# Shared k/q buffer, two accumulators, one PSUM tile for den and num, and a split first wave in a fused attention and gated FFN kernel

## Chip, cores and metric

One core of one Trainium2 chip. The metric is device time in microseconds (us), the median over several executions. All kernels here were checked against the reference and were correct.

## The reference, cut to what matters

Polynomial sketch attention over 4 batches of 4 heads and 1088 rows, followed by a gated FFN on all 4352 tokens:

```python
def phi(x):                      # r = 8, so 64 features
    a = np.einsum('rd,bhsd->bhsr', S1, x)
    b = np.einsum('rd,bhsd->bhsr', S2, x)
    return np.einsum('bhsi,bhsj->bhsij', a, b).reshape(*x.shape[:-1], r * r)
q_p, k_p = phi(q), phi(k)
kv  = np.einsum('bhsf,bhsd->bhfd', k_p, v)
z   = np.sum(k_p, axis=2)
num = np.einsum('bhsf,bhfd->bhsd', q_p, kv)
den = np.einsum('bhsf,bhf->bhs', q_p, z)[..., None] + 1e-06
x   = num / den                  # then (B,H,S,D) -> (B*S, 128)
gate = 1.0 / (1.0 + np.exp(-(x @ w_gate)))          # d_ff = 1536
out  = (gate * (x @ w_val)) @ w_out
```

## The kernel before

TensorE does FFN *waves* (gate and value product of one block of 128 FFN columns, for 512 tokens) and *output matmuls*, and the attention of the next batch is slipped in between them with `slot(group, waves)`. den and num stand in tiles of two different PSUM pools:

```python
    def den(b, n):
        dps = ps1.tile([P, 512], F32, tag="one", name="dps")
        for h in range(H):
            nc.tensor.matmul(out=dps[32 * h : 32 * h + 32, :w], ...)
        def invert():
            nc.vector.transpose(out=dT[:, :tn]..., in_=dps[:, :w])
            ...                                    # rc, reciprocal, rb
        return invert

    def num(b, n):
        nps = ps2.tile([P, 2, 512], F32, tag="two", name="nps")
        ...                                        # 4 heads x 2 halves of matmuls
        def divide():                              # xT <- nps * rb
            ...
        return divide
```

Names in the profile lines: kT and qT are k and q transposed; kps and cqps are the matmuls that sketch k and q; qp and bq are the two factors of the features of q, written to DRAM (dq) and read back repeated, and their product goes into qp. kvz, ndps, zb and nd lead to kv and z. dT is den transposed, rc its reciprocal, rb the reciprocal spread out, and xT the quotient that the FFN reads. sg is the sigmoid, g the gated product, moeout the output accumulator.

The order on the queues for a batch, and the narrowing of weights to float32 (`w_sb`), of which the last step needs a square from ScalarE and a sum from GpSimd:

```python
    def num0_den1(b):
        divide = num(b, 0)
        invert = den(b, 1)
        divide()
        invert()
    ...                                            # for batches 1 to 3
        qmult(b, 0)                                # qp <- qp * bq (bq: repeated operand)
        slot(lambda: ndt(b), wn)
        qmult(b, 1)
        slot(lambda: den(b, 0)(), wn)
        slot(lambda: num0_den1(b), wn + 1)
        slot(lambda: num(b, 1)(), 3)

        # in narrow():
        nc.scalar.activation(out=cap.bitcast(F32), in_=cap.bitcast(F32), func=ACTF.Square)
        nc.gpsimd.tensor_tensor(out=head, in0=head, in1=tail, op=ALU.add)
        yield
        nc.vector.scalar_tensor_tensor(
            out=out, in0=cap.bitcast(F32), scalar=1.265625 * 2.0**-30, in1=head.bitcast(F32), ...)
```

Of the kernel before, what the change touches and what calls it, by code (L numbers as in the profile page):

```python
# [9 lines left out]
I32 = mybir.dt.int32  # L10
# [10 lines left out]
def kernel(  # L21
# [42 lines left out]
    ps1 = ctx.enter_context(tc.tile_pool(name="ps1", bufs=1, space=bass.MemoryType.PSUM))  # L64
# [18 lines left out]
    def narrow(out, bits, eng):  # L83




        n, m = out.shape[1:]
        lo, hi = bits[:, :, :, 0].bitcast(U32), bits[:, :, :, 1]

        def tmp(dt, tag, bufs):
            return sbN.tile([P, 3, P], dt, tag=tag, name=tag, bufs=bufs)[:, :n, :m]



        cap, tail = tmp(I32, "cap", 5), tmp(I32, "tail", 4)
        eng.tensor_scalar(  # L97
            out=cap.bitcast(F32), in0=hi.bitcast(F32), scalar1=122880.0, scalar2=-122880.0,
            op0=ALU.min, op1=ALU.max,
        )  # L100
        nc.scalar.activation(out=tail, in_=lo, func=ACTF.Copy, scale=2.0**-29)  # L101
        yield

        head = tmp(I32, "head", 3)
        nc.vector.tensor_scalar(  # L105
            out=head, in0=cap, scalar1=3, scalar2=0x3FFFFFF8,
            op0=ALU.logical_shift_left, op1=ALU.bitwise_and,
        )
        nc.vector.scalar_tensor_tensor(  # L109
            out=head, in0=cap, scalar=-0x40000000, in1=head, op0=ALU.bitwise_and, op1=ALU.bitwise_or  # L110
        )
        yield
        nc.scalar.activation(out=cap.bitcast(F32), in_=cap.bitcast(F32), func=ACTF.Square)  # L113
        nc.gpsimd.tensor_tensor(out=head, in0=head, in1=tail, op=ALU.add)  # L114
        yield

        nc.vector.scalar_tensor_tensor(  # L117
            out=out, in0=cap.bitcast(F32), scalar=1.265625 * 2.0**-30, in1=head.bitcast(F32),
            op0=ALU.is_ge, op1=MUL,
        )  # L120
        yield
# [39 lines left out]
    def narrow_w(j, step):  # L161
        if not 0 <= j < NJ:
            return
        n, jj = divmod(j, 2)
        if wide:
            if step == 0:
                narrowing[j] = narrow(w_sb[:, :, j, :], w_in[n][:, :, jj], nc.gpsimd)
            next(narrowing[j])


    def load_rows(src, b, tag, parts=((0, T, nc.sync),), t=None):
        if t is None:
            t = ld.tile([P, T, D], F32, tag=tag, name=tag)
# [9 lines left out]
        return t  # L183
# [16 lines left out]
    k_t[0] = load_rows(k, 0, "k", ((0, KBASE[2] + 1, nc.scalar), (KBASE[2] + 1, T, nc.sync)))  # L200
    q_t[0] = load_rows(q, 0, "q", ((0, T0, nc.sync),))
    v_t[0] = load_v(0)
    load_w(0)
    load_rows(q, 0, "q", ((T0, T, nc.sync),), q_t[0])
    for n in range(1, 4):
        load_w(n)

    def load_kq(b):
        if b < B:
            k_t[b] = load_rows(k, b, "k")  # L210
            q_t[b] = load_rows(q, b, "q")

    k_t[1] = load_rows(k, 1, "k")
    for n in range(4, NJ // 2):
        load_w(n)
    v_t[1] = load_v(1)
    q_t[1] = load_rows(q, 1, "q")
# [32 lines left out]
    def w2(ci, j0, jn, g):  # L250
        t0, tw = tok_chk[ci]
        if j0 == 0:
            moe["acc"] = pso.tile([P, TCH], F32, tag="moeout", name="moeout")
# [33 lines left out]
    def w1():  # L287
# [6 lines left out]
        for which in range(2):  # L294
            for jj in range(jn):
                nc.tensor.matmul(  # L296
                    out=wv[:, which, jj * tw : (jj + 1) * tw],
                    lhsT=w_sb[:, which, j0 + jj, :],
                    rhs=xT[:, t0 : t0 + tw],
                    start=True,  # L300
                    stop=True,
                )
        sg = sbG.tile([P, TCH], F32, tag="sg", name="sg", bufs=3)
        nc.scalar.activation(out=sg, in_=wv[:, 0], func=ACTF.Sigmoid)  # L304
        if ci == 0:
            narrow_w(j0 + 4, 0)
            if j0 == 0:
                narrow_w(1, 3)
            narrow_w(j0 + 2, 1)
            narrow_w(j0 + 2, 2)  # L310
            if j0 > 0:
                narrow_w(j0 + 1, 3)
# [18 lines left out]
    def slot(group, waves):  # L331
# [4 lines left out]
        for _ in range(waves):  # L336
# [7 lines left out]
            lag = 3 if last or todo and todo[0][1] == 0 and todo[0][0] > 0 else 2  # L344
            while len(todo) >= lag:
                w2(*todo.pop(0))
                lag = 3 if last else 2
# [115 lines left out]
    def qcomp(b, ns, pool):  # L463
# [23 lines left out]
        BQ[b] = sbA.tile([P, H * TP * 32], F32, tag="bq", name="bq", bufs=1)  # L487
# [44 lines left out]
    def kv(b, j_list, zsum=None):  # L532

        if b not in KVZ:
            KVZ[b] = ps1.tile([P, 512], F32, tag="one", name="kvz")
        kvz = KVZ[b]
        for j in j_list:
            kr = 64 if j == 0 else P
            for which in range(2 if zsum is None else 1):
                for h in range(H):  # L540
                    nc.tensor.matmul(  # L541
                        out=kvz[32 * h : 32 * h + 32, F * which : F * which + F],
                        lhsT=v_t[b][:kr, h, j, :] if which == 0 else ones[:kr, :],
                        rhs=KP[b][:kr, h // 2, j, h % 2, :],
                        start=(j == 1 and which == 0),
                        stop=(j == 0),
                        skip_group_check=True,
                    )
        if 0 not in j_list:
            return  # L550
        if zsum is not None:
            for h in range(H):
                nc.tensor.matmul(
                    out=kvz[32 * h : 32 * h + 32, F : 2 * F],
                    lhsT=ones,
                    rhs=zsum[:, h, :],
                    start=False,
                    stop=True,
                    skip_group_check=True,
                )  # L560

        KVD[b] = sbA.tile([P, 2, 2, F], F32, tag="kvd", name="kvd")
        k0 = kvz[:, : 2 * F]
# [25 lines left out]
    def ndt(b, pool=(ps1, "one")):  # L589
        ndps = pool[0].tile([P, 2, 256], F32, tag=pool[1], name="ndps")  # L590
# [16 lines left out]
    def den(b, n):  # L607
        t0, tn = q_chk[n]
        w = 32 * tn
        dps = ps1.tile([P, 512], F32, tag="one", name="dps")  # L610
        for h in range(H):
            nc.tensor.matmul(  # L612
                out=dps[32 * h : 32 * h + 32, :w],
                lhsT=zb[b % 2][:, h, :],
                rhs=half(QP[b], n)[:, 2 * (h % 2) + h // 2, :],
                start=True,
                stop=True,
            )

        def invert():  # L620

            dT = sbA.tile([P, 9, 32], F32, tag="dT", name="dT")
            nc.vector.transpose(out=dT[:, :tn].rearrange("p t c -> p (t c)"), in_=dps[:, :w])  # L623
            rc = sbA.tile([P, 9, 2], F32, tag="rc", name="rc")
            nc.vector.tensor_scalar_add(rc[:, :tn], dT[:, :tn, :2], 1e-6)
            nc.vector.reciprocal(out=rc[:, :tn], in_=rc[:, :tn])

            rb = sbA.tile([P, 9, 2, 32], F32, tag="rb", name="rb")
            r0 = rc[:, :tn]
            nc.vector.transpose(  # L630
                out=rb[:, :tn].rearrange("p t c s -> p (t c s)"),
                in_=bass.AP(
                    tensor=r0.tensor, offset=r0.offset, ap=[list(r0.ap[0]), [1, 2 * tn], [0, 32]]
                ),
            )
            RB[b, n] = rb

        return invert

    def num(b, n):  # L640
        t0, tn = q_chk[n]
        w = 32 * tn
        nps = ps2.tile([P, 2, 512], F32, tag="two", name="nps")
        for h in range(H):
            for c in range(2):
                rows = slice(64 * c, 64 * c + 64)
                nc.tensor.matmul(  # L647
                    out=nps[32 * h : 32 * h + 32, c, :w],
# [6 lines left out]
        def divide():  # L655
            o = b * S + 64 * t0
            nc.vector.tensor_tensor(  # L657
                out=xT[:, o : o + 2 * w].rearrange("p (t c s) -> p c t s", c=2, s=32),
                in0=nps[:, :, :w].rearrange("p c (t s) -> p c t s", s=32),
                in1=RB[b, n][:, :tn].rearrange("p t c s -> p c t s"),  # L660
                op=MUL,
            )
            moe["ready"] = o + 2 * w
# [40 lines left out]
    for j0, j1 in ((0, 5), (5, NJK)):  # L704
        for pi in range(2):
            outer(0, pi, j0, j1)
        if j0 == 0:
            kv(0, [1, 2, 3, 4])
    narrow_w(0, 0)
    kv(0, [5, 6, 7, 8, 0])  # L710
    narrow_w(1, 0)
    mult00()
    narrow_w(0, 1)
    mult10()
    narrow_w(0, 2)
    ndt(0, (pso, "moeout"))
    warm(256)
    narrow_w(0, 3)
    invert = den(0, 0)
    divide = num(0, 0)  # L720
    warm(512)
    narrow_w(2, 0)
    narrow_w(3, 0)
    invert()
    divide()
    narrow_w(1, 1)
    narrow_w(1, 2)
    turn_q(0, 1)
# [10 lines left out]
    def num0_den1(b):  # L739
        divide = num(b, 0)  # L740
        invert = den(b, 1)
        divide()
        invert()

    def q01():
        spread(0, (1,), qcomp(0, (1,), (ps2, "two")), nc.scalar, True)

    slot(q01, 6)
    qmult(0, 1)
    slot(None, 2)  # L750
    slot(lambda: den(0, 1)(), 1)
    slot(lambda: num(0, 1)(), 1)
    for b in range(1, B):
# [7 lines left out]
        load_kq(b + 1)  # L761
# [6 lines left out]
        slot(lambda: kv(b, [1, 2, 3, 4, 5, 6, 7, 8, 0], ZS[b]), wn)  # L768
# [5 lines left out]
        slot(lambda: den(b, 0)(), wn)  # L774
        slot(lambda: num0_den1(b), wn + 1)
        slot(lambda: num(b, 1)(), 3)
# [31 lines left out]
```

## Time and profile before

| | before |
|---|---|
| time, median of 3 (range); a fourth execution came with the result | 315.51 us (314.66 to 316.38) |
| span of the profiled execution | 313.1 us, granted clock 0.999 |
| TensorE busy | 300.3 us (96%) |
| first wave starts | 18.05 us |
| two gaps before an output matmul, both for g | 1.33 us at 40.92, 1.13 us at 81.41 |

TensorE is the bound, so what counts is where it waits. From its timeline alone: a wave takes 1.715 us when nothing holds it, an output step of two matmuls 0.8575 us, and there are 102 of each, 262.4 us in all.

### The profile page before, as it was taken

How to read it: one execution, taken by the hardware profiler on the slowest of the kernel's cores; microseconds unless marked ns; L12 is line 12 of the kernel's file. 1: busy time of each engine (PE TensorE's matmuls, PEld its weight loads, DVE VectorE, ACT ScalarE, POOL GpSimd, SP SyncE). 2: the span in 40 equal slices, each digit the busy share in tenths (PEclk: the TensorE clock that was granted, in tenths of full speed). 3: DMA queues.
4: the chain of work that ended last, by engine and by line, in shares of the span. 5: the costliest groups of instructions: out<-in, count | busy, mean ns of one | idle time of the engine just before them, and what ended most of it. 6: DMA issues, size and time to landing. Idle time of an engine off the chain costs nothing.

```text
span 313.1 us, 3666 instructions
## 1 busy us (share of the span) xinstructions
PE 300.3 (96%) x1394; PEld 135.5 (43%) x1394; DVE 155.0 (49%) x259; ACT 80.9 (26%) x149; POOL 21.2 (7%) x34
## 2 busy tenths in 40 slices
PE   7889989999799999999999999999999999999994
PEld 2423423453244444543443444433444444444683
DVE  4888798843827444465246451653332223222331
ACT  2445532321122122212222222312122222222220
POOL 1256621000000000000000000000000000000000
PEclk9999999999999999999999999999999999999999
DMA  7996302596204393220003750110002000200011
GB/s 180 345 380 200 118 1 75 149 158 128 66 0 108 101 171 119 60 51 1 2 0 55 173 116 13 16 20 0 0 0 34 0 2 2 32 0 0 8 28 17
DMA packets 28656, 22.91 MB, mean 73 GB/s; under 512 B 19808, under 2 KB 23776, under 8 KB 28640
## 3 DMA queue, kind: packets, MB, share of 16 engines
q1 hardware_dynamic: 27712, 22.14, 28.3%
q10 hardware_dynamic: 928, 0.54, 0.7%
q8 instruction: 11, 0.18, 0.2%
q14 instruction: 5, 0.04, 0.0%
HBM read 19.46 MB, written 3.21 MB: 72 GB/s over the span
## 4 chain that ended last, share of the span: by engine, by line
PE 77%; DMA 11%; DVE 5%; SPq 4%; issue 1%; POOL 1%; ACT 1%; DVEq 0%; POOLq 0%; ACTq 0%
PE wave L296 48%; PE moeout L256 25%; DMA bq<-dq 7%; DMA w_in<-in_moe_w_out_dram 2%; DMA dq<-cq 2%; SPq L515 2%; PE nps L647 1%; PE dps L612 1%; DVE qp L530 1%; PE kvz L541 1%; DVE w_sb L117 1%; POOL head L114 1%; DVE g L317 1%; SPq L189 1%; DVE head L109 1%
## 5 line engine op out<-in xcount | busy, mean ns | idle before, releaser
L296 PE MATMUL wave<-xT,w_sb 128*128 128x512 f32 (+1 forms) x432 | 191.4, 570 | 1.5 <-DVE w_sb L117 1.2
L317 DVE TENSOR_TENSOR g<-wave,sg 128x512 f32<-128x512 f32 x102 | 70.2, 688 | 125.7 <-ACT sg L304 125.3
L296 PEld LDWEIGHTS wave<-xT,w_sb 128*128 128x128 f32 x432 | 81.4, 190 | 96.4 <-issue 85.1
L304 ACT ACTIVATE sg<-wave 128x512 f32<-128x512 f32 x102 | 60.9, 597 | 206.7 <-PE wave L296 205.2
L256 PE MATMUL moeout<-g,w_sb 128*128 128x512 f32 (+1 forms) x216 | 104.6, 577 | 2.5 <-DVE g L317 2.5
L256 PEld LDWEIGHTS moeout<-g,w_sb 128*128 128x128 f32 x216 | 39.2, 189 | 47.2 <-issue 36.9
L114 POOL TENSOR_TENSOR head<-head,tail 128x384 int32<-128x384 int32 (+1 forms) x13 | 13.7, 1053 | 18.8 <-DVE head L109 15.1
L530 DVE TENSOR_TENSOR qp<-qp,bq 128x1152 f32<-128x1152 f32 (+1 forms) x7 | 9.0, 1291 | 7.4 <-DMA bq<-dq 7.4
L657 DVE TENSOR_TENSOR xT<-nps,rb 128x512 f32<-128x512 f32 (+1 forms) x8 | 5.8, 722 | 10.2 <-PE nps L647 10.1
L404 DVE TENSOR_TENSOR kp<-kab 128x1152 f32<-128x1152 f32 (+2 forms) x10 | 10.7, 1092 | 0.0
L109 DVE SCALAR_TENSOR_TENSOR head<-cap,head 128x384 int32<-128x384 int32 (+1 forms) x13 | 7.3, 565 | 0.4
L229 PE MATMUL warm<-ones 128*128 128x512 f32 (+1 forms) x10 | 6.7, 796 | 1.0 <-DVE hm L235 1.0
L113 ACT ACTIVATE cap<-cap 128x384 f32<-128x384 f32 (+1 forms) x13 | 6.5, 499 | 3.8 <-DVE head L109 3.8
L101 ACT ACTIVATE tail<-w_in 128x384 int32<-128x384 uint32 x12 | 6.5, 552 | 3.2 <-DMA w_in<-in_moe_w_out_dram 3.2
L117 DVE SCALAR_TENSOR_TENSOR w_sb<-cap,head 128x384 f32<-128x384 f32 x12 | 6.9, 579 | 0.8 <-POOL head L114 0.8
L97 POOL TENSOR_SCALAR cap<-w_in 128x384 f32<-128x384 f32 x12 | 6.5, 548 | 7.1 <-DMA w_in<-in_moe_w_out_dram 7.1
L105 DVE TENSOR_SCALAR head<-cap 128x384 int32<-128x384 int32 (+1 forms) x13 | 6.6, 508 | 0.7 <-POOL cap L97 0.7
L541 PEld LDWEIGHTS kvz<-kp,v 128*32 128x32 f32 (+1 forms) x288 | 5.3, 109 | 3.3 <-issue 2.7
L266 DVE STREAM_TRANSPOSE o_sb<-moeout 128x512 f32<-128x512 f32 (+1 forms) x9 | 6.1, 677 | 1.3 <-PE moeout L256 1.3
L647 PE MATMUL nps<-qp,nd 64*32 64x256 f32 (+1 forms) x128 | 6.1, 401 | 0.6 <-issue 0.6
L541 PE MATMUL kvz<-kp,v 128*32 128x64 f32 (+1 forms) x288 | 6.5, 221 | 0.1
L612 PE MATMUL dps<-qp,zb 128*32 128x256 f32 (+1 forms) x64 | 5.3, 404 | 1.3 <-DVE dT L623 0.7
(55 smaller groups left out, 75.5 us busy)
## 6 DMA issues: line engine op xcount, KB each, us to landing
v<-in_v_dram SPq DMA_DIRECT2D x16, 144.0 KB
bq<-dq SPq DMA_DIRECT2D x8, 288.0 KB
qp<-dq SPq DMA_DIRECT2D x3, 576.0 KB
k<-in_k_dram SPq DMA_DIRECT2D x3, 544.0 KB
q<-in_q_dram SPq DMA_DIRECT2D x3, 544.0 KB
w_in<-in_moe_w_gate_dram SPq DMA_DIRECT2D x6, 256.0 KB
w_in<-in_moe_w_val_dram SPq DMA_DIRECT2D x6, 256.0 KB
w_in<-in_moe_w_out_dram SPq DMA_DIRECT2D x6, 256.0 KB
```

The costliest lines, as they stand in the source:

```text
L109: nc.vector.scalar_tensor_tensor(out=head, in0=cap, scalar=-0x40000000, in1=head, op0=ALU.bitwise_and, op1=ALU.bitwise_or)
L114: nc.gpsimd.tensor_tensor(out=head, in0=head, in1=tail, op=ALU.add)
L117: nc.vector.scalar_tensor_tensor(out=out, in0=cap.bitcast(F32), scalar=1.265625 * 2.0**-30, in1=head.bitcast(F32), op0=ALU.is_ge, op1=MUL,)
L256: nc.tensor.matmul(out=moe["acc"][:, :tw], lhsT=w_sb[:, 2, j, :], rhs=g[:, jj, :tw], start=(j == 0), stop=(j == NJ - 1),)
L296: nc.tensor.matmul(out=wv[:, which, jj * tw : (jj + 1) * tw], lhsT=w_sb[:, which, j0 + jj, :], rhs=xT[:, t0 : t0 + tw], start=True, stop=True,
L304: nc.scalar.activation(out=sg, in_=wv[:, 0], func=ACTF.Sigmoid)
L317: nc.vector.tensor_tensor(out=g, in0=wv[:, 1], in1=sg, op=MUL)
L404: nc.vector.tensor_tensor(out=KP[b][:, pi, j0:j1].rearrange("p j m (i l) -> p (j m) i l", i=R), in0=bass.AP(tensor=a0.tensor, offset=a0.of ...
L530: nc.vector.tensor_tensor(out=q0, in0=q0, in1=half(BQ[b], n), op=MUL)
L541: nc.tensor.matmul(out=kvz[32 * h : 32 * h + 32, F * which : F * which + F], lhsT=v_t[b][:kr, h, j, :] if which == 0 else ones[:kr, :], rh ...
L612: nc.tensor.matmul(out=dps[32 * h : 32 * h + 32, :w], lhsT=zb[b % 2][:, h, :], rhs=half(QP[b], n)[:, 2 * (h % 2) + h // 2, :], start=True, ...
L647: nc.tensor.matmul(out=nps[32 * h : 32 * h + 32, c, :w], lhsT=ND[b][rows, 32 * h : 32 * h + 32], rhs=half(QP[b], n)[rows, 2 * (h % 2) + h ...
```

## The change

The intent was: bq (the repeated operand) takes the place of k and q in one buffer, so that SBUF and early transfers are saved; two accumulator banks let a chunk start before the last one is read out; den and num in one PSUM tile free a bank and keep den and num together; the first wave starts as soon as half its tokens are there; the square of the narrowing goes to PSUM, so that VectorE's last step has one SBUF input less. The core of the diff:

```diff
+        square = cap.bitcast(F32)
+        if psum:
+            square = pso.tile([P, 512], F32, tag="acc1", name="square")[:, : n * m]
-            moe["acc"] = pso.tile([P, TCH], F32, tag="moeout", name="moeout")
+            moe["acc"] = pso.tile([P, TCH], F32, tag=f"acc{ci % 2}", name="moeout")
-        BQ[b] = sbA.tile([P, H * TP * 32], F32, tag="bq", name="bq", bufs=1)
+        BQ[b] = ld.tile([P, 2, T, D], F32, tag="kq", name="bq").rearrange("p a t d -> p (a t d)")
+        tp = tw // 2 if ci == 0 and j0 == 0 else tw          # first wave in two halves
+        for o in range(0, tw, tp): ...
-    def den(b, n): ... dps = ps1.tile([P, 512], F32, tag="one", name="dps") ...
-    def num(b, n): ... nps = ps2.tile([P, 2, 512], F32, tag="two", name="nps") ...
+    def dn(b, n):
+        t = ps2.tile([P, 2, 512], F32, tag="two", name="dn")
+        ...   # den into t[:, i, w:], then num into t[:, :, :w]
+        def divide(*parts):
+            ...   # dT <- t[:, i, w:], rc, then rb and xT part by part
-    invert = den(0, 0)                                        # the start of batch 0
-    divide = num(0, 0)
+    narrow_0(...)       # gate and value third of block 0 first, output third later
+    divide = dn(0, 0)
+    divide((0, 4), (4, 8))
-        load_kq(b + 1)                                        # early in the batch
-        slot(lambda: den(b, 0)(), wn)
-        slot(lambda: num0_den1(b), wn + 1)
-        slot(lambda: num(b, 1)(), 3)
+        load_kq(b + 1)                                        # after the last use of bq
+        slot(lambda: dn(b, 0)(), wn)
+        slot(None, 1)
+        slot(lambda: dn(b, 1)(), 4)
```

kv of batch 0 moved into an accumulator bank too, and its matmuls were reordered; the transpose of q and the second cqps of batch 0 came two waves later. In the waves of the first chunk (the first 512 tokens) the last narrowing step of the next block now comes ahead of the other narrowing steps, and the output step of a chunk's first wave no longer lags by one wave more.

## The prediction

> **What bounds the kernel now.** I read the page first: its busy line, slices and chain of work.
>
> ```profile
> PE 300.3 (96%) x1394; PEld 135.5 (43%) x1394; DVE 155.0 (49%) x259; ACT 80.9 (26%) x149; POOL 21.2 (7%) x34
> PE   7889989999799999999999999999999999999994
> ...
> DVE  4888798843827444465246451653332223222331
> ...
> PE 77%; DMA 11%; DVE 5%; SPq 4%; issue 1%; POOL 1%; ACT 1%; DVEq 0%; POOLq 0%; ACTq 0%
> ```
>
> TensorE is the bound, and from about 96 us on it is full. The gated FFN alone is 306 matmuls of 512 columns (8.5 chunks of 36); in the timeline a wave of two takes 1.72 us, so one is 0.858 us and all are 262.5 us. The change removes none of these. What can be won is the 18.05 us before the first wave, the gaps among the waves, and small attention matmuls. The 11% of DMA in the chain says that the early gaps come from transfers. So I read the timeline of TensorE and looked for waits. First the start, then the two large gaps:
>
> ```profile
> 18.05 1.98 PE L296 MATMUL wave<-xT,w_sb 128*128 128x512 f32 x4
> ...
> 21.06 1.96 PE L296 MATMUL wave<-xT,w_sb 128*128 128x512 f32 x4 [0.41 <-DVE w_sb L117]
> ...
> 24.50 1.99 PE L296 MATMUL wave<-xT,w_sb 128*128 128x512 f32 x4 [0.63 <-DVE w_sb L117]
> ...
> 40.92 1.13 PE L256 MATMUL moeout<-g,w_sb 128*128 128x512 f32 x2 [1.33 <-DVE g L317]
> ...
> 81.41 1.13 PE L256 MATMUL moeout<-g,w_sb 128*128 128x512 f32 x2 [1.13 <-DVE g L317]
> ```
>
> Taking start-to-start times against 1.72 us a wave and 0.86 us an output matmul, TensorE loses 0.8 us at 22.9 to 24.5, 2.0 us at 37.7 to 42.3 and 2.1 us at 78.2 to 82.4. The timeline of VectorE shows what stands behind the last two: it sits in its queue at the product with the repeated operand, with the g that TensorE needs queued behind it.
>
> ```profile
> 38.90 1.36 DVE L530 TENSOR_TENSOR qp<-qp,bq 128x1152 f32<-128x1152 f32 x1 [1.36 <-DMA bq<-dq]
> 40.18 0.68 DVE L317 TENSOR_TENSOR g<-wave,sg 128x512 f32<-128x512 f32 x1
> ...
> 77.82 1.36 DVE L530 TENSOR_TENSOR qp<-qp,bq 128x1152 f32<-128x1152 f32 x1 [4.33 <-DMA bq<-dq]
> ```
>
> **What the Trainium skill says.** (1) "SBUF — State Buffer", Who interferes with whom: a VectorE instruction with two SBUF inputs contends with a GpSimd instruction that reads SBUF, and the loser waits. The trace agrees: the last narrowing step (two SBUF inputs, 384 elements) takes 0.88 us at 20.03, beside a GpSimd operation, and 0.55 us in most other places. Squares in PSUM leave it one SBUF input. (2) "VectorE: DVE Perf Modes", Why PSUM operands drop a tier: no fp32 PSUM source is above one element per cycle; but this step has two tensors and is at that rate already, so PSUM costs it little. No run here shows it yet. (3) "Perfetto Trace Analysis", Optimizing Tensor Performance: rotate matmul groups through different PSUM banks. The trace shows no loss that two accumulators would mend: around the change of chunk at 132 us waves and outputs follow in 1.72 us and 0.86 us steps. (4) "DMA: Bandwidth & Descriptors", Issuing engines are not separate DMA queues: all transfers share 16 engines, so moving k and q may relieve the repeated operand. Below the trace says: hardly, once the pipeline runs.
>
> **The change part by part.**
>
> *Start, worth about 1.2 us at the third wave.* The instruction order shows gate and value weights of the first block narrowed alone (256 elements), the output third later, kv ahead of it, and the division in two halves. Before, kv ends at 12.7, its copy at 13.1, ndps at 13.7, but zb waits until 14.25 because VectorE does a narrowing and a product first; w_sb ends at 15.47, dT starts at 15.5, xT ends at 17.99. After: the third outer product still ends at 11.2, the two products end at 12.4, the 256-element head steps at 13.1, zb at 13.8; nd and square follow on ScalarE to 14.5, w_sb to 14.95, dT starts at 15.0 to 15.1. Then dT 0.45, rc and reciprocal 0.45, half an rb 0.4, half an xT 0.4: the first half wave can start near 16.9 instead of 18.05, the second half at 17.7. But wave two needs w_sb of block 1, whose chain (head 0.9, GpSimd add 1.0, w_sb 0.5) begins only after xT: 17.6 + 2.5 gives 20.2, against 21.06. Wave three gains more, since its last narrowing step no longer queues behind the next block's two head steps (1.7 us in the timeline at 22.29 to 23.9): about 23.3 against 24.5. Then cqps now stands here and a 0.77 us transpose of q on VectorE too, and wave four starts near 26.8 against 27.3.
>
> *The first repeated operand, worth 2.0 us.* Before, cqps follows wave one and the product comes after seven waves; now it follows wave three, six waves before the product, but with half a chain less in front. cq is copied near 27, dq is written in about 3.5 us (before 5.0 us, with k, v and q of batch 1 in the queue), reads are issued near 31 and land 10.6 us later as before: 41.4 us. Waves 5 to 9 run at 2.57 us from 29.4; VectorE reaches the product near 41.3 and ends it near 42.8. TensorE first needs it for den after wave ten, near 44.0. So the 2.0 us gap closes. After that g and two accumulators bring nothing more.
>
> *Shared buffer: free, with slack.* k and q of batch 1 are read only after the product, 42.8 us. Before, the same loads for batch 2, issued at 51.6 and 53.5, had their last packets at 55.0 and 57.7. So k lands near 46.8 and q near 48.5. The transpose of k comes on VectorE three waves later, near 49.6. Slack about 3 us. In later batches there are six and more waves (15 us) for it. By then cqps of batch 1 stands near 54.1 us, as before, but with one wave and one output matmul more behind it: 2.57 us ahead.
>
> *den and num in one tile, loses about 1.0 us in batch 1.* TensorE work stays: den and num stand together (one change of operand less, about 0.2 us a batch), den of the second half is split into 224 and 64 columns (four more matmuls of a few tens of ns). But the order on VectorE moves: before it was product, dT, rc, reciprocal, rb, g, xT; now xT (0.7 us) is ahead of g too. cqps ends at X; the product's data come at X + 23.1 (77.8 - 54.7), and eight waves with outputs (20.6), kv 1.7, ndps 0.2 and den with num 1.5 bring TensorE to the g at X + 24.2. VectorE: 1.36, then 0.45, 0.2, 0.25, 0.7, 0.7 and 0.65 give X + 27.35. So a gap of 3.1 us, where there are 2.1 us. Batches 2 and 3 have two waves per step and no such wait.
>
> *Sum.* 2.6 us won by 54 us, 1.0 lost near 80, some 0.3 won in fewer operand changes: 1.9 us, 315.5 - 1.9 = 313.6 us. The tail (308.8 to 313.1) is untouched.
>
> **The rivals.** (A) Removing k and q of batch 2 from ahead of the reads lets the repeated operand of batch 1 come early, and that gap closes: 3 us more, 310.5 us. Against it: last packets come 16.6, 15.4 and 16.2 us after the first read issue in batches 1, 2 and 3 (issues at 60.1, 106.4 and 172.8), and batch 3 has no k or q load beside it; so the length is the reads' own. For it: k and q of batch 2 were still moving until 57.7, while dq was being written. I give it a quarter. (B) The late load of k and q is exposed, or heads the sync queue behind a wait: each microsecond beyond the slack is one on the path, 315 to 317 us. The order on the queue shows the v loads ahead of the reads with their wait long met; I give it a tenth. (C) VectorE is so full in the first chunk (31.1 of 36.7 us between 18.0 and 54.7) that the waves are paced by head, add, w_sb, and the start gain is eaten: then 314.5 us. Squares on one PSUM buffer, which ScalarE cannot refill before VectorE has read it, would add to it. A fifth.
>
> **Range and chances.** A pulls the centre down more than B and C push it up; I set 313.0 us. The runs of before spread 1.7 us. All gaps together (0.4 + 0.8 + 2.0 + 2.1) and 1.5 us of start would be 6.8 us, just beyond the 6.3 us that make 2%: nearly every part must work in full, so 0.1. Slower by 2% needs a new stall of 8 us: 0.02.
>
> **What would show it.** Right: the first wave near 17 and the third near 23.3; no wait of over 0.5 us on g near 40; the product of batch 1 still waiting for bq near 78, and TensorE idle 2.5 to 3.5 us for g there. Wrong: kT or qT of batch 1 waiting for the k or q load (B); the gap near 80 gone (A), which would be the largest error downward; waves of the first chunk over 2.7 us apart waiting for w_sb (C).

## More of the kernel before

A verdict is "faster" or "slower" when the whole 95% interval of the ratio lies beyond 2%, "same" when it lies within 2%, and "unclear" when it crosses that line. The rounds ran on different chips, so kernels of different rounds are compared by their ratios to the kernel before, which ran in each of them.

At the start, with all engines in the timeline (start, duration, engine, line, operation, out<-in):

```profile
15.50 0.45 DVE L623 STREAM_TRANSPOSE dT<-dps 128x256 f32<-128x256 f32 x1
...
16.50 0.63 PE L647 MATMUL nps<-qp,nd 64*32 64x256 f32 x6 [0.56 <-issue]
...
17.30 0.69 DVE L657 TENSOR_TENSOR xT<-nps,rb 128x512 f32<-128x512 f32 x1
```

The transpose of den (dT) starts at 15.50, while the last matmuls of num run until 17.13. The chain dT, reciprocal, rb is hidden behind num.

The kps matmuls open the attention of batches 1, 2 and 3. From the start of each of them I take off the waves and output steps that lie before it. What is left is the time outside the FFN at full rate: start, attention, gaps and slow stretches. For the kernel before: 53.55 us minus 12 waves and 10 outputs gives 24.40 us up to batch 1, then 8.63 for batch 1, 6.37 for batch 2 and 11.3 for the rest.

## The result, and the profile after

| | before | after |
|---|---|---|
| time, median of 4 (range) | 315.4 us (314.66 to 316.38) | 323.66 us (322.95 to 324.36) |
| ratio after to before, 95% interval | | 1.026 (1.0224 to 1.0296) |
| span and clock of the profiled execution | 313.1 us, 0.999 | 321.8 us, 0.993 |

A ratio here is the mean time of one kernel's fast runs over that of the other's of the same rounds, so it is not quite the ratio of the medians quoted. All outputs are right. The page of after: busy line, granted clock in 40 slices, chain of work that ended last.

```profile
PE 303.6 (94%) x1430; PEld 138.7 (43%) x1430; DVE 155.5 (48%) x268; ACT 80.4 (25%) x151; POOL 21.3 (7%) x36
...
PEclk9999999999979999999999999999999999999999
...
PE 78%; DVE 10%; DMA 6%; issue 2%; SPq 1%; ACT 1%; POOL 1%; ACTq 0%; DVEq 0%
```

VectorE's share of the chain has doubled from 5% to 10% although its busy time is the same; DMA fell from 11% to 6%. One slice has a granted clock of 7 tenths; before, all were 9. The view of waits, first before, then after (engine, line, what it waited for: total, times, longest), shows which instruction is behind it:

```profile
PE moeout L256 <- DVE g L317: 2.5, 2, 1.3
...
DVE dT L623 <- PE dps L612: 2.0, 2, 1.4
```

```profile
DVE dT L665 <- PE dn L654: 14.0, 6, 5.3
...
PE moeout L266 <- DVE g L329: 8.7, 8, 3.9
```

dT, the transpose of den, waited for den's matmuls (L612) before. Now it waits for L654, which is **num**, not den (L644). And TensorE waits eight times for g, 8.7 us in all, where there were two waits and 2.5 us. The start of after in the timeline:

```profile
16.65 0.63 PE L654 MATMUL dn<-qp,nd 64*32 64x256 f32 x6 [0.42 <-issue]
...
17.33 0.45 DVE L665 STREAM_TRANSPOSE dT<-dn 128x256 f32<-128x256 f32 x1 [1.14 <-PE dn L654]
...
19.36 1.96 PE L309 MATMUL wave<-xT,w_sb 128*128 128x256 f32 x8 [1.02 <-DVE xT L684]
...
21.03 0.99 POOL L117 TENSOR_TENSOR head<-head,tail 128x384 int32<-128x384 int32 x1 [5.13 <-DVE head L104]
21.05 1.12 DVE L108 SCALAR_TENSOR_TENSOR head<-cap,head 128x128 int32<-128x128 int32 x1
...
22.79 1.95 PE L309 MATMUL wave<-xT,w_sb 128*128 128x512 f32 x4 [1.46 <-DVE w_sb L120]
...
23.51 0.63 DVE L120 SCALAR_TENSOR_TENSOR w_sb<-cap,head 128x128 f32<-128x128 f32 x1 [0.87 <-ACT tail L100]
```

dT starts 0.05 us after the last matmul of num ends, 1.8 us later than before, and the first wave comes at 19.36 instead of 18.05, although it needs only half its tokens. Two things follow it. The head step of the output third, 128 columns, takes 1.12 us beside a GpSimd operation that started 0.02 us before it (the same step on 384 columns took 0.56 us at 20.32), and holds up w_sb of the second wave. The last step of that third waits 0.87 us on VectorE, so g and the first output matmul come late too: the second wave is at 22.79 (before 21.06), the third at 26.82 (24.50), the fourth at 30.32 (27.30). In batch 1:

```profile
83.04 1.36 DVE L541 TENSOR_TENSOR qp<-qp,bq 128x1152 f32<-128x1152 f32 x1 [4.97 <-DMA bq<-dq]
...
86.64 1.28 DVE L329 TENSOR_TENSOR g<-wave,sg 128x512 f32<-128x512 f32 x2
```

```profile
87.38 1.12 PE L266 MATMUL moeout<-g,w_sb 128*128 128x512 f32 x2 [3.94 <-DVE g L329]
88.34 3.23 PE L309 MATMUL wave<-xT,w_sb 128*128 128x512 f32 x4
...
96.55 1.13 PE L266 MATMUL moeout<-g,w_sb 128*128 128x512 f32 x2 [0.65 <-DVE g L329]
```

TensorE stands 3.94 us for g (before 1.13). Then four matmuls of a wave take 3.16 us to the next start (den at 91.50), where 1.81 us are normal ahead of den, in the slice of the low clock. A third, shorter gap follows at 96.55, after the second half of den and num. Batch 2, where the prediction saw no wait:

```profile
147.71 0.45 DVE L665 STREAM_TRANSPOSE dT<-dn 128x256 f32<-128x256 f32 x1 [1.16 <-PE dn L654]
...
157.58 0.55 DVE L665 STREAM_TRANSPOSE dT<-dn 128x224 f32<-128x224 f32 x2 [2.60 <-PE dn L654]
```

Behind them TensorE waits 0.41 us at 150.78 and 0.65 us at 160.89 for g; the same pair comes back in batch 3 at 215.12 and 225.22. Before had neither.

The table of the time outside the FFN (us) puts the loss in its places. It also has the experiments, which follow:

| kernel | to batch 1 | batch 1 | batch 2 | rest | span |
|---|---|---|---|---|---|
| before | 24.4 | 8.6 | 6.4 | 11.3 | 313.1 |
| after | 26.4 | 12.9 | 7.75 | 12.35 | 321.8 |
| after (r_after_again) | 26.0 | 11.6 | 7.75 | 12.3 | 320.0 |
| e1_den_own_bank | 25.65 | 10.65 | 6.5 | 11.1 | 316.3 |
| e2_den_num_apart | 25.3 | 8.1 | 6.4 | 10.9 | 313.1 |
| e3_shared_kq_alone | 24.3 | 8.3 | 6.4 | 11.3 | 312.7 |
| e9_dn_alone | 27.7 | 9.0 | 7.75 | 12.25 | 319.1 |
| e6_old_start | 24.2 | 11.7 | 7.7 | 11.9 | 317.9 |
| e7_fill_gap | 26.5 | 10.5 | 7.7 | 12.3 | 319.5 |
| e5_one_bank | 29.3 | 11.5 | 7.7 | 12.3 | 323.2 |
| e4_square_sbuf | 29.25 | 13.0 | 7.75 | 12.4 | 324.8 |
| e10_best | 24.6 | 6.5 | 6.5 | 10.6 | 310.7 |
| e11_best_psum | 22.5 | 6.5 | 6.5 | 10.6 | 308.6 |

The loss of after is 2.0 + 4.3 + 1.4 + 1.05 = 8.7 us, the difference of the spans.

### The profile page after: what moved, and what is told of

Read it like the earlier page. It is cut to its first block, busy times and chain, and to the rows that moved or that the text cites. A ratio compares the mean times of both kernels' runs of the same rounds, so it can differ in the third digit from the quotient of the medians.

```text
span 321.8 us, 3740 instructions
## 1 busy us (share of the span) xinstructions
PE 303.6 (94%) x1430; PEld 138.7 (43%) x1430; DVE 155.5 (48%) x268; ACT 80.4 (25%) x151; POOL 21.3 (7%) x36
## 3 DMA queue, kind: packets, MB, share of 16 engines
q1 hardware_dynamic: 27712, 22.14, 27.7%
## 4 chain that ended last, share of the span: by engine, by line
PE 78%; DVE 10%; DMA 6%; issue 2%; SPq 1%; ACT 1%; POOL 1%; ACTq 0%; DVEq 0%
PE wave L309 46%; PE moeout L266 25%; DMA bq<-dq 5%; DVE rb L675 2%; DVE xT L684 2%; DVE g L329 2%; PE dn L654 1%; PE dn L644 1%; DVE dT L665 1%; DMA kq<-in_k_dram 1%; PE kvz L551 1%; PE kps L396 1%; SPq L526 1%; PE kvz L565 1%; DVE head L108 1%
## 5 line engine op out<-in xcount | busy, mean ns | idle before, releaser
L117 POOL TENSOR_TENSOR head<-head,tail 128x384 int32<-128x384 int32 (+3 forms) x14 | 13.4, 959 | 22.4 <-DVE head L108 12.0
L120 DVE SCALAR_TENSOR_TENSOR w_sb<-square,head 128x384 f32<-128x384 f32 x11 | 6.1, 555 | 4.4 <-POOL head L117 4.4
L108 DVE SCALAR_TENSOR_TENSOR head<-cap,head 128x384 int32<-128x384 int32 (+3 forms) x14 | 7.9, 565 | 0.5
L96 POOL TENSOR_SCALAR cap<-w_in 128x384 f32<-128x384 f32 (+2 forms) x13 | 7.0, 549 | 4.1 <-DMA w_in<-in_moe_w_val_dram 4.1
L100 ACT ACTIVATE tail<-w_in 128x384 int32<-128x384 uint32 (+2 forms) x13 | 6.5, 518 | 0.0
L654 PE MATMUL dn<-qp,nd 64*32 64x256 f32 (+1 forms) x128 | 6.1, 401 | 0.4 <-issue 0.4
L675 DVE STREAM_TRANSPOSE rb<-rc 128x576 f32<-128x576 f32 (+2 forms) x9 | 6.1, 680 | 0.3
L684 DVE TENSOR_TENSOR xT<-dn,rb 128x576 f32<-128x576 f32 (+2 forms) x9 | 6.0, 661 | 0.3
L384 DVE STREAM_TRANSPOSE qT<-kq 128x512 f32<-128x512 f32 (+1 forms) x8 | 5.7, 714 | 0.0
L644 PE MATMUL dn<-qp,zb 128*32 128x256 f32 (+2 forms) x96 | 5.6, 338 | 0.1
## 6 DMA issues: line engine op xcount, KB each, us to landing
qp<-dq SPq DMA_DIRECT2D x3, 576.0 KB, 10.6
```

What stands on the lines that cost most here:

```text
L108: nc.vector.scalar_tensor_tensor(out=head, in0=cap, scalar=-0x40000000, in1=head, op0=ALU.bitwise_and, op1=ALU.bitwise_or)
L644: nc.tensor.matmul(out=t[32 * h : 32 * h + 32, i, w : w + 32 * (u1 - u0)], lhsT=zb[b % 2][:, h, :], rhs=half(QP[b], n)[:, 2 * (h % 2) + h ...
L654: nc.tensor.matmul(out=t[32 * h : 32 * h + 32, c, :w], lhsT=ND[b][rows, 32 * h : 32 * h + 32], rhs=half(QP[b], n)[rows, 2 * (h % 2) + h // ...
L675: nc.vector.transpose(out=rb[:, u0:u1].rearrange("p t c s -> p (t c s)"), in_=bass.AP(tensor=r0.tensor, offset=r0.offset, ap=[list(r0.ap[0 ...
L684: nc.vector.tensor_tensor(out=xT[:, o : o + 64 * (u1 - u0)].rearrange("p (t c s) -> p c t s", c=2, s=32), in0=t[:, :, 32 * u0 : 32 * u1].r ...
```

## The experiments

Theories: **S**, the shared tile: den's transpose must wait until num is done in the same tile, which delays xT and g. **O**, the order: that xT now stands ahead of g on VectorE, and that den and num stand together, is what costs, wherever they lie. **N**, the new start (split narrowing, half wave) costs by itself. **C**, the long gap lets the clock of TensorE fall. **K** and **L**: the shared buffer gains, or its late load is exposed. Two runs ask what squares and accumulators are worth, and two put together what gained.

### e1_den_own_bank: den back in a bank of its own, order unchanged

```diff
 def dn(b, n):
-        for i, u0, u1 in pieces:
-            ... out=t[32 * h : 32 * h + 32, i, w : w + 32 * (u1 - u0)]
+        dps = pso.tile([P, 512], F32, tag=f"acc{(ci + 1) % 2}", name="dps")   # idle accumulator
+            ... out=dps[32 * h : 32 * h + 32, :w]
-                nc.vector.transpose(..., in_=t[:, i, w : w + 32 * (u1 - u0)])
+            nc.vector.transpose(..., in_=dps[:, :w])
 # and the square of the last of the 12 blocks goes back to SBUF, here and in e2
```

> The changed kernel, with den written to the accumulator bank that is idle at the time and num alone in its tile; the order on every queue stays (den, num, then dT, rc, rb, xT, and g after them). Theory S (the shared tile makes the transpose dT wait until num is finished too): dT starts right after den or the product, 1.1 us earlier at the start (it is then held by w_sb, which ends at 16.2) and 0.6 us earlier in each of the six later places where TensorE now waits 0.4 to 1.3 us for g; in batch 1's first division nothing, since the data of bq end last there. Sum 1.1 + 5 x 0.6: about 319.5 us. Theory O (it is the order on VectorE, xT ahead of g, that costs): the gaps before g near 148, 158, 213 and 223 us stay at 0.4 to 0.65 us, and the time stays at 323 us within 1 us.

Measured: 317.17 us (315.58 to 318.52), ratio to before 1.0041 (0.9964 to 1.0118). S is right, and the gain was more than expected. In the view of waits dT now waits for den's matmuls, with the order on the queues as in after:

```profile
DVE dT L663 <- PE dps L643: 9.6, 5, 4.7
...
PE moeout L266 <- DVE g L329: 3.2, 2, 2.3
```

Eight waits of TensorE for g have become two (one of 0.90 us at 24.84 is the other), and the two pairs of 0.41 and 0.65 us in batches 2 and 3 are gone. What is left is the gap of batch 1 (2.31 us) with a slow wave behind it, and a new wait of 1.11 us near 47 us, where den takes the bank that a square of the narrowing still occupies. The edit gives den both a tile and a bank of its own, so it does not tell which of the two made dT wait.

### e2_den_num_apart: also the order of before

```diff
 # on top of e1: den and num as separate groups again, for all but the first half of batch 0
-    slot(lambda: dn(0, 1)(), 2)
+    slot(lambda: den(0, 1)(), 1)
+    slot(lambda: num(0, 1)(), 1)
-        slot(lambda: dn(b, 0)(), wn)
-        slot(None, 1)
-        slot(lambda: dn(b, 1)(), 4)
+        slot(lambda: den(b, 0)(), wn)
+        slot(lambda: num0_den1(b), wn + 1)
+        slot(lambda: num(b, 1)(), 3)
```

> The changed kernel with den and num apart again in the batches, in the order of the kernel before (dT to rb ahead of the next g, xT behind it; den of the second half beside num of the first), den in the idle accumulator bank; start, shared buffer, accumulators and squares as in the changed kernel. If the joint tile with its order is what costs in the batches (S and O together): no wait for g of over 0.3 us after 96 us, the gap near 84 us shrinks from 4.1 to about 2.1 us, the slow wave after it (3.2 us for 1.7) is gone, and the time is 316 to 317.5 us, the rest being the start. If the late load of k and q, or the accumulators and squares, cost the time instead: 321 us or more.

Measured: 316.26 us (314.03 to 317.98), ratio 1.002 (0.9943 to 1.0097): the time is as expected. By the profiles the order costs in batch 1 alone: 8.1 us there, against 10.65 in e1; elsewhere the two agree within 0.4 us. But the profiled execution of e1 has the slow stretch, worth 1.7 us (e7 and r_after_again, below), and that of e2 has not. Nor does e2 seem to be rid of it in every execution, as was expected: two of the four executions of each kernel had a mean clock of 0.991 to 0.995, and were 1.8 to 4.0 us longer than the two others. So the order's own part is nearer 0.9 us, which is also the difference of the medians, with intervals that overlap: O may be a small part, in one place, and is not shown beyond that.

### e3_shared_kq_alone: the kernel before with only the shared buffer

```diff
-        BQ[b] = sbA.tile([P, H * TP * 32], F32, tag="bq", name="bq", bufs=1)
+        BQ[b] = ld.tile([P, 2, T, D], F32, tag="kq", name="bq")...      # k, q and bq: one buffer
     qmult(0, 1)
+    load_kq(1)
```

> The kernel before with the shared buffer alone: k and q of a batch in one tile that bq takes over, so that k and q of the next batch are loaded after the second product; v of batch 1 too comes after the second num of batch 0 in the program. Theory K (the shared buffer pays by clearing the queue ahead of the first repeated operand): the wait of VectorE for bq near 39 us (1.4 us) and TensorE's 2.0 us gap go, the transposes of k of batch 1 do not wait by more than 1.5 us, and the time is 313.5 us, 0.994 of before. Rival L (the late load is exposed and takes the place of the wait): 316 us or more with a wait for k of over 2 us near 50 us.

Measured: 314.41 us (313.5 to 315.26), ratio 0.9965 (0.9908 to 1.0022). No transpose of k or q of batches 1 to 3 waits for its load, so L is refuted. The wait for the first repeated operand fell from 1.36 to 0.52 us and TensorE's gap there from 1.33 to 0.54. The gain of about a microsecond that K expects is inside the interval, but so is none.

### e6_old_start: after with the start of before

```diff
-        tp = tw // 2 if ci == 0 and j0 == 0 else tw
+        tp = tw
-    narrow_0(0, 0) ... narrow_0(1, 2)           # block 0 in two pieces
-    divide((0, 4), (4, 8))
+    narrow_w(0, 0) ... narrow_w(0, 3)           # block 0 whole; kv, narrowing, products in the old order
+    divide()
```

> The changed kernel with the start of the kernel before: block 0 narrowed whole with its square in SBUF, kv in two runs over all heads, no halves in the first division and the first wave, same order of narrowing steps; the joint den and num tile stays. Theory N (splitting the narrowing of block 0 and running kv ahead of it cost: its third step waits 0.9 us in VectorE's queue and holds up block 2): the third wave, at 30.3 us for 27.3 before counting the first as one, comes 1.5 to 2 us earlier, and the time is 321.5 to 322 us. Rival (the lateness of the start is only dT waiting for num): the start gains under 0.5 us, or loses by the halves that are gone, and the time is 323.5 us or more.

Measured: 322.41 us (320.12 to 322.84), ratio 1.0204 (1.014 to 1.0269). The first waves start at 19.47, 22.06, 24.71 and 28.10, against 19.36, 22.79, 26.82 and 30.32 in after. dT starts 0.43 us later with the new start (17.33, here 16.90), so of the about 0.5 us that the half division and half wave seem to win, 0.1 is left at the first wave, and both are within the spread of starts (below); the third wave lost 2.1. By the stages N is right: the old start gives back 2.2 us of the 8.7 (column "to batch 1": 26.4 to 24.2). The times alone would not show it: the ratio's interval overlaps that of after, and the verdict against before is unclear. The profiled execution was the shortest of the four, so only its start is read here.

### e9_dn_alone: the kernel before with only the joint tile

```diff
-    def den(b, n): ... ; def num(b, n): ...
+    def dn(b, n): ...                          # as in the changed kernel
-        slot(lambda: den(b, 0)(), wn)
-        slot(lambda: num0_den1(b), wn + 1)
-        slot(lambda: num(b, 1)(), 3)
+        slot(lambda: dn(b, 0)(), wn)
+        slot(None, 1)
+        slot(lambda: dn(b, 1)(), 4)
```

> The kernel before with den and num in one tile alone, in the changed kernel's order (den, num, dT, rc, rb, xT, then g); everything else is the kernel before. Theory S (the joint tile is the cause of the loss by itself): the same waits for g appear as in the changed kernel (0.4 and 0.65 us in batches 2 and 3, 3 to 4 us and a slow wave in batch 1), 1.4, 1.1 and 3.5 to 4.3 us in the three later batches, and about 1 us before the first wave: 321 to 323 us, 1.02 of before. Rival (the joint tile hurts only together with the shared buffer and the new start): 317 us or less.

Measured: 323.96 us (321.27 to 324.4), ratio 1.0257 (1.0196 to 1.0317): the joint tile, with its order on the queues, alone costs by the medians as much as the whole change. dT and the waves of its timeline:

```profile
17.52 0.45 DVE L636 STREAM_TRANSPOSE dT<-dn 128x256 f32<-128x256 f32 x1 [1.76 <-PE dn L625]
...
20.09 1.95 PE L296 MATMUL wave<-xT,w_sb 128*128 128x512 f32 x4 [1.55 <-DVE xT L655]
...
91.38 1.12 PE L256 MATMUL moeout<-g,w_sb 128*128 128x512 f32 x2 [0.65 <-DVE g L317]
```

L625 is num. dT is 2.0 us later than before (17.52 for 15.50) and so is the first wave (20.09 for 18.05). The waits of 0.4 and 0.65 us are in batches 2 and 3 as in after; batch 2 costs the same 7.75 us. That the totals agree is partly chance. In the stages e9 loses 3.3, 0.4, 1.4 and 1.0 us where after loses 2.0, 4.3, 1.4 and 1.05: its gap in batch 1 was 1.71 us with no slow stretch, and, without the shared buffer, VectorE still waits for the first repeated operand. The profiled execution was the shortest of the four and at clock 0.997; the others took 323.6 to 324.4 us at 0.992.

### e7_fill_gap: four idle matmuls in the gap of batch 1

```diff
         slot(lambda: dn(b, 0)(), wn)
+        if b == 1:
+            fill(4)          # 4 products of ones with 512 columns, into the idle accumulator, unused
         slot(None, 1)
```

> The changed kernel with four idle 512-column matmuls on ones into the idle accumulator bank, placed in the gap of batch 1 where TensorE waits 3.9 us for g; nothing else is moved. Theory C (the wave after the gap is slow, 3.2 us for 1.7, because TensorE had been idle and its granted clock fell to 0.8 in that slice): the wave takes 1.9 us or less, the slice shows full clock, and the time falls by about 1.4 us to 322.2 us, though the wait for g stays. Rival (the wave is slow for another reason, such as a wait that is not recorded): the wave still takes over 3 us, and the time is 323.6 us or more.

Measured: 321.16 us (320.57 to 321.51), ratio 1.0184 (1.0132 to 1.0236), where after had 1.026. Four matmuls were added (3.44 us from the first of them to the next output step) and the time fell, by about 2 us in the medians, though the intervals of the ratios overlap; the verdict against before is unclear. The windows of TensorE (stretch, its length, busy time and count, granted clock, DMA share, GB/s), first after, then e7:

```profile
84.00:88.00 4.00, 0.62 (x2) 1.00 1.01 271
88.00:92.00 4.00, 4.00 (x14) 0.59 0.25 99
```

```profile
84.00:88.00 4.00, 4.00 (x10) 1.00 0.48 194
88.00:92.00 4.00, 4.00 (x39) 1.00 0.00 0
```

Without the filling, the clock granted after the gap is 0.59; with it, it is full, and batch 1 takes 10.5 us outside the FFN for 12.9 and 11.6. C is right. The four executions of e7 had clocks 0.998 to 1.0, those of after 0.992 to 0.995. Cut finer, the trace of after shows a clock of 0.50 for 3.41 us, from 88.73 to 92.14, and 1.00 on both sides. Half of 3.41 is 1.7 us of matmul time lost.

### e5_one_bank and e4_square_sbuf: accumulators and squares

e5 undid two parts at once, so its result alone is ambiguous; e4 undid one of them.

```diff
 # e5_one_bank
-            moe["acc"] = pso.tile([P, TCH], F32, tag=f"acc{ci % 2}", name="moeout")
+            moe["acc"] = pso.tile([P, TCH], F32, tag="acc0", name="moeout")
 # e5_one_bank and e4_square_sbuf
-                narrowing[j] = narrow(w_sb[:, :, j, :], w_in[n][:, :, jj], nc.gpsimd, True)
+                narrowing[j] = narrow(w_sb[:, :, j, :], w_in[n][:, :, jj], nc.gpsimd)
```

> The changed kernel with one accumulator bank for the FFN (the other is left for ndps of batch 0) and the squares of the narrowing back in SBUF, so two parts of the change undone together. If both parts are worth nothing on the path, as predicted: 323.6 us within 1 us, no wait of a first output matmul for the transpose of the accumulator over 0.5 us. If the second bank hides the transposes: up to 0.7 us at each of eight changes of chunk, 326 us or more. If squares in PSUM cost (ScalarE waits for VectorE to read the last one): 322 us or less, with the waves of the first chunk closer together.

> The changed kernel with only the squares moved back into SBUF; two accumulators stay. It separates the two changes that the kernel with one accumulator undid together. If the squares in PSUM are what the first chunk's waves gain from: time 1.0 to 1.5 us above the changed kernel, 324.8 us, with waves of the first chunk 2.9 us apart and waits for w_sb. If the second accumulator was what counted: 323.6 us, the same as the changed kernel.

Measured: e5 325.01 us (321.51 to 325.38), ratio 1.0274 (1.0199 to 1.0349). e4 326.03 us (323.14 to 327.62), ratio 1.0315 (1.0265 to 1.0365), beside 1.0243 for after on the same chip (below): 2.7 us between the medians, more than expected, with intervals that overlap a little. With squares in SBUF, one accumulator instead of two is not slower, so no run here shows the second accumulator by itself to be worth anything. The squares in PSUM are. The step that reads the square, as a group (count, then busy us, mean ns, idle time before it), in e4 between 17 and 54 us:

```profile
L120 DVE SCALAR_TENSOR_TENSOR w_sb<-cap,head 128x384 f32<-128x384 f32 x10 | 8.2, 817 | 4.6 <-POOL head L117 4.6
```

and in e11, which has squares in PSUM:

```profile
L120 DVE SCALAR_TENSOR_TENSOR w_sb<-square,head 128x384 f32<-128x384 f32 x10 | 5.6, 558 | 5.5 <-POOL head L117 5.5
```

One such step of each, beside the GpSimd operation that starts just before it. In e4 it is stretched by 0.32 us:

```profile
35.51 0.53 POOL L96 TENSOR_SCALAR cap<-w_in 128x384 f32<-128x384 f32 x1
35.58 0.88 DVE L120 SCALAR_TENSOR_TENSOR w_sb<-cap,head 128x384 f32<-128x384 f32 x1 [0.61 <-POOL head L117]
```

In e11, beside the same operation, it is not:

```profile
35.31 0.54 POOL L96 TENSOR_SCALAR cap<-w_in 128x384 f32<-128x384 f32 x1
35.38 0.56 DVE L120 SCALAR_TENSOR_TENSOR w_sb<-square,head 128x384 f32<-128x384 f32 x1 [0.60 <-POOL head L117]
```

The step is on the path there: in e4 four waves in a row start 2.95 us apart (36.51, 39.46, 42.43, 45.38), in e11 2.57 us (34.11, 36.69, 39.26, 41.84). e11 differs from e4 in more than the squares; after, which differs from e4 in them alone, has the same mean (555 ns) and the same 2.57 us (35.47, 38.04, 40.62, 43.19).

### e10_best and e11_best_psum: the parts that gain, together

e10 is the start of before, the shared buffer, two accumulators whose idle one takes den, den and num apart in this order, and squares in SBUF. e11 puts the squares of all of the 12 blocks but the first and the last back into PSUM (its expectation says blocks 1 to 7, which is a slip: they are 1 to 10).

```diff
 # e10, on top of e2 with the start of before
         qmult(b, 0)
         slot(lambda: ndt(b), wn)
-        qmult(b, 1)
         slot(lambda: den(b, 0)(), wn)
-        slot(lambda: num0_den1(b), wn + 1)
-        slot(lambda: num(b, 1)(), 3)
+        slot(lambda: num(b, 0)(), wn)
+        qmult(b, 1)                   # the long wait for bq now behind den, num and g
+        load_kq(b + 1)
+        slot(None, 1)
+        slot(lambda: den(b, 1)(), 1)
+        slot(lambda: num(b, 1)(), 2)
 # e11, on top of e10
-                narrowing[j] = narrow(..., nc.gpsimd)
+                narrowing[j] = narrow(..., nc.gpsimd, 0 < j < NJ - 1)
```

> A version meant to beat both: shared buffer and later cqps of the changed kernel; den and num apart, den in the idle accumulator bank; start of the kernel before; squares in SBUF; and the second product with the repeated operand moved behind the first division of the batch, since only the second half needs it. Time outside FFN matmuls, up to kps of batch 1: 23.2 us (24.2 with the old start and the joint tile, less 1 us of waiting dT); batch 1: 6 us (8.1 with den and num apart, less the 2.1 us of the wait for bq); then 6.4 and 11 us as with den and num apart; with 262.4 us of FFN 309 us in the trace and about 311 us, 0.985 of before. If the second product still waits for bq, or the transpose of k of batch 2 now waits for its later load: 313 us or more.

> The best version so far (den in the idle accumulator bank, order of before on the queues, start of before), with the squares of narrowing blocks 1 to 7 put back into PSUM. If squares in PSUM take about 0.2 us off each of the first chunk's waves (as the kernel with one accumulator and squares in SBUF suggested), the last FFN wave of the first chunk comes 1.0 to 1.5 us earlier than in the version with SBUF squares: span 309.5 us, median 312.0. If the PSUM squares are worth nothing, as the prediction had it, span 310.7 and median 313.2.

Measured: e10 313.25 us (312.89 to 313.74), ratio 0.9936 (0.9896 to 0.9977). e11 311.51 us (310.86 to 311.95), ratio 0.9869 (0.9837 to 0.9901). Both beat both kernels; neither beats before by 2%. e10 missed its expectation by 2 us, at the start: 24.6 us to batch 1, not 23.2. No product waits for bq in it. The span of e11 is 2.1 us below that of e10, and all of it is before batch 1 (24.6 to 22.5 in the table). In both the gap of batch 1 is gone (6.5 us for 8.6), because the product that waits for bq no longer stands ahead of g.

### r_after_again: the changed kernel a second time

> The changed kernel again, beside the others on the same chip, and to see whether the slow wave after the long gap of batch 1 (clock digit 7 in one slice) comes back: about 323.6 us, slower than before by 2.6 per cent, and the wave after the gap again near 3.2 us with a clock below 0.9 in that stretch. If the slow wave was an accident of one execution, the clock is full there and the span near 320.2 us.

Measured: 323.34 us (321.73 to 325.09), ratio 1.0243 (1.0201 to 1.0285). No edit. The slow stretch comes back, after a gap of 2.54 us:

```profile
85.61 2.00 PE L266 MATMUL moeout<-g,w_sb 128*128 128x512 f32 x2 [2.54 <-DVE g L329]
87.40 2.75 PE L309 MATMUL wave<-xT,w_sb 128*128 128x512 f32 x4
```

The output step of two matmuls takes 1.79 us to the next start, where 0.96 us are normal after a gap, and the wave 2.68 us, where 1.81 are normal ahead of den: 1.7 us lost again. So it was no accident. The gap itself varies with the landing of bq: 3.94 us in one execution, 2.54 in the other.

## Why the prediction was wrong

It foresaw 313.0 us and no change; the kernel became 2.6% slower. By its own steps:

- **Start, 1.2 us won at the third wave: wrong.** The step that failed is "dT starts at 15.0 to 15.1". dT started at 17.33, and the first wave at 19.36 instead of 16.9. Both the joint tile and the new start are in this. About 1.2 us come from the steps ahead: zb started at 14.54, not 13.8, the square on ScalarE ended at 15.55, not 14.5, and w_sb at 16.2, not 14.95. The other 1.1 us are the wait for num in the joint tile: with den in its own bank (e1) dT follows w_sb at once, at 16.47, and the first wave starts at 18.63. The step "wave three gains more, since its last narrowing step no longer queues" failed too: wave three was at 26.82, not 23.3, because the output third that was moved back became late (1.12 us and 0.87 us above). e6 puts the new start at 2.2 us lost.
- **The first repeated operand, 2.0 us won: right.** The wait is gone: the product starts at 45.91 without waiting for bq, later than the 41.3 worked out, as the whole start is late; with the start of before (e11) it starts at 41.96, again without a wait. But the start took the gain away. Stage by stage: with the shared buffer, PSUM squares and the start of before, e11 is at 22.5 us, 1.9 below before; with the joint tile, e6 is at 24.2; with the new start as well, after is at 26.4.
- **Shared buffer, free: right** (in e3 and in after no wait for k or q of batches 1 to 3).
- **den and num in one tile, 1.0 us lost in batch 1 only: the mechanism in batch 1 was right, the rest was wrong.** VectorE does product, dT, rc, reciprocal, rb, xT, g as worked out, 3.6 us from the product's data at 83.04 to g at 86.64, and the gap (2.54 to 3.94 us in two executions) brackets the 3.1 foreseen. (That sum has a slip: its terms add to X + 24.0 and X + 27.4, so 3.4.) The step that failed is "Batches 2 and 3 have two waves per step and no such wait". They lose 1.4 and about 1.05 us, because there dT waits not for bq but for num, and TensorE then stands 0.41 and 0.65 us for g in each. Nowhere in the prediction's sums does dT wait for num. The Trainium skill gives a reason for such a wait: "PSUM — Partial Sum Buffer", PSUM bank collisions raise a hardware error, has VectorE reading a bank while TensorE writes it, also in other columns, raise an error, and asks to guard by bank and 32-partition quadrant, or simply by bank. The trace shows a wait that fits (dT released by L654), and e1 shows that another tile in another bank lifts it; whether the bank or the tile set it, no run separates. The prediction drew on other sections of the skill and not on this one. Whether a read of den beside num's matmuls would have gone through was not tried, since it would be a race.
- **Not foreseen: the clock.** After the gap of batch 1 the clock fell to half for 3.41 us, 1.7 us lost, in both profiled executions of after; e7 shows no such stretch.
- **PSUM squares, given no worth: wrong. Accumulators worth nothing: right.** The prediction cited the collision of two SBUF inputs with GpSimd, saw 0.88 us for 0.55 us, and put no price on it. In the kernel before the step seldom meets the GpSimd operation (580 ns in the mean). In the order of after it meets it in eight of ten blocks: 817 ns in the mean with squares in SBUF (e4), 555 ns with them in PSUM. So this part pays for another part, the moved last step, and is worth 2.1 us where it can be seen alone (e11 against e10).
- **Rivals.** A: false, the gap near 80 grew, and VectorE still waited 4.97 us for bq there. B: false. C, that VectorE paces the waves of the first chunk: true of the first three waves; from the fourth on, the squares in PSUM keep it off.

The sum of the parts in the stages: foreseen 21.8 us to batch 1 (24.4 - 2.6), measured 26.4; foreseen 9.6 in batch 1, measured 12.9; foreseen nothing beyond, measured 2.4. That is 4.6 + 3.3 + 2.4 = 10.3 us of the 10.6 us between the span that the prediction's sum makes (313.1 - 1.9 = 311.2) and 321.8.

What stays open: how the joint tile's cost splits between tile and bank, and between the wait for num and the order on VectorE (e1 against e2 is within the noise); the first wave of kernels with the same start also varies (18.05, 18.90, 18.05 and 17.71 us in before, e3, e10 and e11), so start differences below a microsecond are not read. How long a gap the clock bears is bracketed only: the six profiled executions with a wait for g of 2.31 to 4.00 us in batch 1 (e1, e5, r_after_again, e6, after, e4) all had the stretch at half clock, 3.41 us long each time; e9 with 1.71 us, and before and e2 with 1.13, had none, at one look each. Three other executions of e9 had a mean clock of 0.992 and may have had one.

## What to carry to other kernels

Before two results are put in one PSUM tile, ask who reads the first while the second is being written: here the reader's whole chain moved behind the second. A wait in the queue of an engine that is half idle (VectorE here) costs as soon as the operand of the bound engine stands behind it; move what waits for a slow transfer behind what TensorE needs, as e10 does. A part that looks worthless alone may pay for another part of the same change, so price each in the order that the others leave.

## What the Trainium skill lacked or had wrong

- "TensorE: Matmul & The Clock Gate", HAM oscillation: it advises against idle gaps of TensorE above about 3.4 us. Here a gap of 2.31 us (e1) and one of 2.54 us (r_after_again) were already followed by a granted clock of 0.64 and 0.72 in the 4 us from 84, and matmuls at about half rate (two in 1.79 us for 0.96); one of 1.71 us (e9) was not. The half rate agrees with the page's idle state. Four matmuls of no use in the gap (e7) kept the clock at 1.0; the page does not name this remedy for a gap inside a kernel.
- "PSUM — Partial Sum Buffer", PSUM bank collisions raise a hardware error: no run here tests the rule. It states no cost of keeping to it: here dT behind num, with the order on the queues that came with it, made the kernel before 2.6% slower when nothing else was changed (e9; interval 1.0196 to 1.0317).
- "SBUF — State Buffer", Who interferes with whom: agrees, but it gives no size. A VectorE step with two SBUF inputs took 817 ns in the mean beside a GpSimd operation (e4), 558 ns with one of the two in PSUM (e11).
- "Perfetto Trace Analysis", Optimizing Tensor Performance: no run here shows a gain of rotating banks for the accumulator by itself (e5 with one bank 1.0274, e4 with two 1.0315 against before); the idle bank gained as a place for den (e1, 1.0041 where after has 1.026).
